# A fused attention and feed-forward kernel whose hand-listed order of operations is replaced by another order

## The chip, the cores and the metric

The kernel runs on one core of a Trainium2 chip. The metric is the device time of one execution in microseconds (us), of which smaller is better. A core has TensorE (PE in the profile, with its weight loads as PEld), VectorE (DVE), ScalarE (ACT), GpSimd (POOL) and SyncE (SP). TensorE writes its products into PSUM, eight banks of accumulators, and only VectorE and ScalarE read them out in this kernel.

## The reference: what is computed

Attention with a squared ReLU in the place of softmax, over 8 batches and 12 heads of 448 rows and 64 columns, and then a feed-forward block with an exact GELU over the 3584 rows of 768 columns:

```python
scores = scale * np.matmul(q, k.transpose(0, 1, 3, 2))
attn = np.maximum(scores, 0.0) ** 2 / S
x = np.matmul(attn, v)        # laid out as 3584 x 768
h = x @ w_in                  # 768 x 2048
g = 0.5 * h * (1.0 + erf(h / sqrt(2)))
out = g @ w_out               # 2048 x 768
```

## The kernel before: how the work is laid out

The kernel first records its work as 1,596 operations of a class `Op` (some of which, like a product, are up to 28 instructions) and then issues them one by one from a table. The kinds that matter here are these.

- **Transposes.** For batches 0 and 1 TensorE turns k and q (`tp`, L619 and L647) and a copy takes them out of PSUM into `kT` and `qT` (L518 when VectorE copies, L520 when ScalarE does). From batch 2 on a DMA on SP's queue turns them (L674).
- **Scores.** A step is four products `ps` of 64x64 blocks (L751), a scaled ReLU out of PSUM into `a_sq` (L768 on ScalarE, or L770 on VectorE) and a squaring on VectorE (L777). Seven steps feed the 28 products `pav` (L824), and two copies take `pav` out into `xT` (L518 or L520).
- **First layer.** Batch 0 uses plain products `psh` (L884) and a GELU (L894). Batches 1 to 6 use a scheme of seven block products in the place of eight (`add_unit`: products `pe` at L1039, copies and additions `part` out of PSUM at L518, L520 and L1077, GELU at L1089). Batch 7 has the like in `add_block` (`pb`, L1190 and L1227).
- **Second layer.** Groups of 256 rows, again with seven block products (`pso`, L1366, additions L1400, sums of operands L1347), and stores on SP's queue (L1319, L1327).

PSUM is divided into two pools. `w_pp` (tag "w") has three tiles of two banks each, here called pairs: a `ps`, a `pav`, a `pe` or a `pb` takes one pair. `f_pp` (tag "f") has two single banks, for `tp`, `psh`, `pso`. An operation marked Q in the table takes the two single banks in the place of a pair (`split`).

In `add_unit` two units of work share each pair. Unit y=0 uses the first bank and unit y=1 the second:

```python
if first and name not in bank:
    bank[name] = w_pp.tile([128, 2, NB], F32, tag="w", name="pe")
...
bank[name][:, y, z * HS : z * HS + HS],
```

Each unit runs product after product into its banks, and the next product into a bank waits for the copy or addition (`passed`) that took the former value out. So there is a chain in each unit: product, copy, product, copy. The other unit's products stand between and give the copy its time. Where the copies of the two units are given to two engines, the built program carries a semaphore wait between them, since both read one tile, the pair: the later of the two in the table waits for the earlier.

The order is a list of words in the table `ORDER` at the top of the file. The letter gives the engine (P and Q TensorE, A ScalarE, D VectorE, G GpSimd, S SyncE, Z a filler on TensorE) and the number the operation. `place()` goes through the words, and `run()` issues the operations in that order, so each engine's instruction stream is the table's words with its letter, read in sequence. Each engine takes its stream strictly in order: an instruction that waits holds back all that stand behind it.

```python
for word in ORDER.split():
    ...
    op, eng = self.open[int(word[1:])], names[word[0]]
    if word[0] == "Q":
        op.split()
```

Of the kernel before, what the change touches and what calls it, by code (L numbers as in the profile page):

```python
# [83 lines left out]
A10 D13 G0 G1594 Z1024 P14 P11 D15 G1 G3 G4 G7 D12 A16 P17 P36 D18 A37 P21 G118 G2 P19 P42 P39 P33  # L84
D22 G117 P23 D20 A43 D40 P48 A34 A49 D24 P25 P54 A55 D26 Z672 P63 P66 D38 A67 D41 D50 P51 A52 P29
D35 P27 D28 D30 D44 P57 D53 D68 P31 D32 A64 A58 P131 P81 G121 A82 P45 A46 A47 P69 A70 D132 D59 G6
P129 P84 A85 P90 A91 G125 G126 D65 G5 D130 P156 D71 D157 P78 A79 Q72 D73 P93 A94 P102 D83 G8 G122
G120 G124 G119 G128 P111 D112 P137 D113 P108 A74 D95 G123 G9 G127 D138 G236 P174 D56 A103 A109 P139
D86 P75 A175 A76 D110 D140 P133 P60 P105 D77 P96 A61 A62 P168 A106 G235 D80 P135 D136 D104 A97 P171
G238 A172 P87 D134 P141 G147 G148 G150 D92 A169 A88 A89 A142 P159 A160 D98 P162 P99 D107 D163 G151  # L90
Q114 A100 A101 P198 A199 D115 D116 P183 A184 P165 A166 D176 P145 A146 S228 S229 G153 P240 A241 D173
D158 G154 D200 P213 A214 P180 D170 A181 P222 P252 A253 D167 S230 P250 A251 D223 P195 D161 A196 P207
D164 D208 P177 P186 A187 D182 D209 D178 D179 P210 D197 P262 A263 D215 A211 G234 P256 P192 D193 P189
P216 P254 A190 A257 S231 P219 A255 D191 D349 D350 D212 P204 A220 P244 S232 S233 D194 A217 P248 A245
A249 D218 D185 P260 A205 P242 A243 D188 P201 A202 D224 G237 G149 G152 A261 G155 D221 D206 P225 D387
D226 D203 A227 D345 D346 D348 P246 A247 D351 P264 G239 G266 P353 P370 A354 P360 P143 A144 G267 P377
P356 D425 D426 A371 D427 A361 A378 D347 P258 A259 D352 P373 D388 P382 P355 A374 P379 D383 D380 P372
P365 A357 P362 D358 P385 A386 D375 A359 D366 D363 P391 P408 A364 G268 P368 A369 P398 P415 P393 P410
D431 A265 D428 A399 D389 P403 D390 A409 A392 P394 D413 P411 A416 P420 D396 D432 A384 A367 P282 Q273
A412 D395 G269 P400 P417 D421 A274 D404 A405 P437 A283 A422 A438 P276 A277 D433 S453 D418 D401 S454  # L100
D434 P291 D429 D435 A292 P406 P423 A424 D430 A407 A402 P439 G270 P288 A289 P285 A286 D293 P297 D298
D440 P441 A442 P315 A316 P279 D284 A414 D287 D436 P300 D290 P443 D444 D275 A280 D281 P445 P447 D278
P309 A301 D446 D448 S451 A397 G271 P303 A419 A381 P294 A376 D469 D470 S455 A310 D295 A304 S456 S457
S458 D305 P312 D311 P449 D450 S452 A313 D302 D314 A296 P321 D471 A322 D323 P324 A325 P306 A307 D308
D317 P473 A474 P339 G459 P327 A328 P475 P477 P336 D299 G462 D472 A340 D329 D476 A337 D338 A478 P330
P318 A331 G272 P333 D334 A319 A320 D332 P479 P498 A499 P492 G465 D341 P489 A490 P481 A493 P495 A496
D335 D326 P342 A343 P507 P504 A505 D480 D482 P485 D344 D561 D562 D564 D563 A508 P565 G460 G461 D509
P582 A583 P572 P589 D494 P585 D586 P567 P584 D500 A566 P568 D573 P591 D570 A590 D592 P594 D587 P577
D599 A569 P483 D578 G463 P601 A588 P618 D486 D595 A602 P574 P597 A598 G464 D600 D491 G466 G467 D575
P603 A576 P620 D484 D619 S488 P580 A581 S635 D606 D497 Q501 A593 S636 A502 S637 D623 P604 P621 D506  # L110
D503 A622 P608 P625 A624 A605 D651 D652 P513 A514 D515 Q510 P522 P610 S638 A596 P627 D626 D628 G641
G644 A609 P613 D611 D653 P630 A511 A512 A523 A571 D614 Q516 A517 P519 D520 P616 P633 D631 A632 D654
D524 A617 P655 A634 P657 P528 D656 D529 P531 A532 D533 S487 G468 P549 A550 D658 P659 D521 A607 D518
P543 A544 P540 A660 D541 P537 A538 P661 P663 D662 A579 D539 P694 P555 D530 D551 A629 P525 A612 A526
D664 A695 D545 D527 P665 D666 A556 D542 P667 A615 D671 P709 A710 D672 P534 P546 S669 P706 A547 D535
A536 A707 P675 D668 P677 P552 S639 S640 G647 P703 D696 P691 D673 G642 D676 D674 D678 P679 A680 D553
A692 P681 D548 D557 P697 D554 P558 G643 G645 G646 D708 A704 P715 D698 P700 D682 D559 P683 A701 D560
P767 P784 D684 D763 A716 D785 A768 D705 D764 P687 P769 P786 P774 D711 D766 P787 A788 D765 A775 D772
P685 A773 G648 D693 D688 D789 G649 S690 P770 A771 D699 P791 D686 P779 A790 Q727 D728 P724 S837 S838
A792 D702 A725 P793 P776 D794 A795 P796 P803 P820 D777 S839 P799 S840 A778 G843 P782 D801 D797 A800  # L120
A783 D804 S670 Q712 P718 G846 D821 D780 A798 A719 A713 A714 P805 P822 P806 D802 P823 D825 A824 Q748
P721 D808 P810 D729 P827 A807 P812 D726 A749 A828 D722 P757 Q730 P829 A811 D717 D853 D854 D830 S689
D813 A731 S841 P832 D833 P857 D858 A826 P818 D732 P815 A809 P835 D720 D816 D855 A831 A819 P859 D860
A758 D759 P861 A817 D862 A836 A834 P896 A897 P733 P739 D740 P863 D856 A734 P742 P905 A906 P745 P865
D898 D864 D866 G650 P867 D735 D750 A781 P869 D868 D723 D870 S872 A814 D873 D874 S842 A746 D747 P920
A921 P736 A737 D738 P751 D876 A743 D744 A752 D753 P877 P879 P911 P754 A878 D880 D875 D741 P908 A755
D756 P881 A882 D909 A912 D922 P883 P893 D894 D884 P899 A900 D910 D895 P760 P926 A761 A762 P923 A924
P885 D886 G849 P887 P902 D913 D901 G844 D888 D965 A927 D967 A903 P917 D907 P889 D890 P969 P986 G845
G847 G848 A918 S1039 D904 Q935 D936 P929 A970 A930 P914 A915 A916 Q941 P971 P988 D966 D968 D919 P976
P993 D925 A987 D991 G850 A994 D937 P972 P989 A990 D977 G851 P981 S892 S1040 D974 A942 P998 A973  # L130
D1003 P1005 P1022 D999 A1000 A1023 P978 D982 D979 A1006 P1007 P1024 D1027 P1008 A992 S1041 A980 Q932
D1010 P995 A1028 P1025 A1026 A933 D996 A997 D1009 P1012 P1029 A1030 D1004 D934 P1014 P1031 D1032
A975 D1013 P1001 A1002 D1015 P1059 D1060 P984 A1016 A985 D931 A1033 S871 G1045 P1020 P1037 A1038
P1034 D1057 P1017 A1021 P950 P1098 P1063 D1055 D1056 D1018 S891 A983 D1035 D951 S1042 S1043 G1048
A1019 P1061 P959 A1099 D1100 P956 D928 D1062 A957 D960 A1036 P938 A939 A940 P1101 D1102 P944 A945
D1058 D946 P1065 A1064 P947 P953 P1119 A1011 D1066 D961 P1067 D958 G852 A948 D1068 A1120 P1069 D943
P1095 A954 D955 D1070 A1096 D1097 D949 D1075 D952 P1122 P1125 A1126 S1073 A1123 P1071 D1072 D1076
P1079 D1080 P1128 D1078 S1074 P1107 A1108 P962 D963 A964 P1110 P1081 D1082 P1083 A1129 A1084 P1104
D1077 D1111 S1044 G1051 G1046 P1113 A1114 P1085 P1173 D1112 A1105 D1106 D1169 P1087 D1109 P1190
P1171 P1188 A1172 A1189 D1086 D1088 P1091 D1103 D1167 D1168 P1178 D1170 D1176 D1092 P1195 A1196  # L140
P1089 P1174 P1191 D1193 A1194 D1130 D1090 Q1134 A1177 A1135 D1115 P1116 D1124 D1179 D1127 A1192
Q1143 D1117 P1183 D1118 A1144 P1200 P1137 A1138 D1175 Q1131 D1201 D1184 A1185 G1047 G1049 P1197
P1180 A1132 A1202 G1050 D1205 D1181 A1182 D1198 D1206 S1241 P1207 P1224 D1208 P1209 P1226 A1225
Q1155 A1156 A1199 P1186 D1212 P1210 D1229 D1145 P1203 A1230 A1204 D1133 P1227 D1228 A1211 P1214
P1231 A1187 P1216 P1233 Q1146 D1139 A1213 D1121 A1232 A1147 D1136 P1140 A1141 Q1149 A1142 D1215
P1219 P1236 D1217 A1218 D1234 A1235 D1150 D1237 A1238 P1222 P1239 G1052 D1220 S1242 Q1152 A1223
D1153 A1240 G1053 A1221 P1270 A1271 P1279 A1280 S1093 S1094 P1276 P1251 A1252 P1158 P1161 D1247
S1243 D1248 A1277 P1253 D1249 D1162 D1157 A1159 P1255 D1254 D1160 P1257 S1244 D1148 D1256 P1259
P1267 P1273 A1274 D1163 D1154 D1151 D1258 D1260 A1268 D1250 P1164 A1165 D1278 P1285 D1281 A1166
D1339 D1340 P1263 A1286 S1245 P1345 P1343 P1360 A1361 P1350 D1272 P1367 P1362 D1287 D1342 D1344  # L150
A1351 P1346 A1368 P1363 A1364 P1372 A1347 D1365 P1261 A1366 D1341 D1275 D1348 P1352 P1369 D1370
D1353 P1355 D1356 S1246 G1595 P1379 P1396 G1054 P1358 D1373 A1371 A1357 D1262 P1375 A1374 A1380
D1377 D1378 P1381 P1398 D1264 D1384 A1397 P1382 P1399 A1359 A1376 A1383 P1386 P1403 A1349 D1401
# [1551 lines left out]
```

## Time and profile before

| | |
|---|---|
| time, median of 3 runs | 365.86 us (365.82 to 366.21) |
| profiled execution, its own time | 365.36 us |
| its span, first to last instruction | 363.5 us |
| mean granted TensorE clock | 0.999 |
| instructions in the span | 9,137 |
| chain that ended last: TensorE | 83% of the span |
| chain that ended last: VectorE, ScalarE, DMA | 8%, 4%, 2% |

The profiled execution is 0.50 us faster than the median of the three timed runs, of which 1.9 us lie outside the span. A row of the timeline gives a start from the span's first instruction, a duration, the engine, the line of the kernel, the operation, its output and input with their shapes, and how many instructions were merged into the row. In brackets stand the idle time ahead of it on its engine and what ended that. A row of the waits view gives who waited for whom, the sum, the count and the longest. A row of the windows view gives, for a stretch of time, the length and then busy time and number of instructions for PE, PEld, DVE, ACT and POOL, and last the TensorE clock, the DMA share and GB/s.

### The profile page before, as it was taken

What the parts mean: (1) busy time and instruction counts of PE and PEld (TensorE: products, weight loads), DVE (VectorE), ACT (ScalarE), POOL (GpSimd) and SP (SyncE); (2) the same over time, 40 slices, a digit from 0 to 9 for tenths busy, and PEclk for the clock granted to TensorE, in tenths of its full rate; (3) what the DMA queues carried; (4) which work ended last, traced back from release to release, by engine and by line L of the source; (5) the groups of instructions that cost most, each with busy time, mean ns of one, the idle gap of its engine ahead of it and who ended that gap; (6) DMA issues with size and microseconds to landing.
All of it is one profiled execution on the core that took longest, in us unless ns stands there. A gap on an engine that the chain in (4) does not pass through costs nothing.

```text
span 363.5 us, 9137 instructions
## 1 busy us (share of the span) xinstructions
PE 352.7 (97%) x3805; PEld 244.2 (67%) x3805; DVE 312.9 (86%) x544; ACT 233.4 (64%) x396; POOL 102.9 (28%) x138
## 2 busy tenths in 40 slices
PE   8889999999999999999999999999999999999995
PEld 4557569855588655886557975678669855798663
DVE  3999988999789899899999799899896999687753
ACT  4998844899846795567675869457854885344200
POOL 8565715284192105610074100470100000000000
PEclk9999999999999999999999999999999999999999
DMA  9999999999999808997199941699900201021213
GB/s 176 200 200 204 202 204 155 172 143 168 155 161 173 157 21 107 142 208 107 56 81 167 183 74 45 94 129 181 136 2 0 88 2 44 3 88 43 88 43 132
DMA packets 124361, 43.01 MB, mean 118 GB/s; under 512 B 102688, under 2 KB 120992, under 8 KB 124320
## 3 DMA queue, kind: packets, MB, share of 16 engines
q0 software_dynamic: 85328, 22.47, 66.4%
q1 hardware_dynamic: 38448, 19.50, 26.3%
q8 instruction: 30, 0.49, 0.6%
q10 hardware_dynamic: 544, 0.46, 0.4%
q14 instruction: 11, 0.09, 0.1%
HBM read 45.61 MB, written 11.01 MB: 156 GB/s over the span
## 4 chain that ended last, share of the span: by engine, by line
PE 83%; DVE 8%; ACT 4%; DMA 2%; issue 1%; POOL 1%; DVEq 0%; POOLq 0%; ACTq 0%
PE pso L1366 36%; PE pe L1039 21%; PE ps L751 8%; PE pav L824 8%; PE psh L884 5%; PE pb L1190 4%; DVE a_sq L777 2%; DMA nq<-in_q_dram 2%; DVE part L1077 2%; DVE part L518 2%; ACT part L520 2%; ACT h_sb L1089 1%; ACT a_sq L768 1%; DVE qT L518 1%; DVE ws L955 0%
## 5 line engine op out<-in xcount | busy, mean ns | idle before, releaser
L768 ACT ACTIVATE a_sq<-ps 128x896 bf16<-128x896 f32 (+1 forms) x151 | 121.9, 861 | 26.1 <-PE ps L751 25.3
L777 DVE TENSOR_TENSOR a_sq<-a_sq 128x896 bf16<-128x896 bf16 x169 | 98.2, 615 | 1.9 <-ACT a_sq L768 1.5
L1366 PEld LDWEIGHTS <-s_sb 128*128 128x128 bf16 x456 | 42.5, 98 | 31.9 <-issue 6.0
L1039 PEld LDWEIGHTS <-win_sb 128*128 128x128 bf16 x576 | 54.4, 98 | 7.9 <-issue 6.3
L751 PE MATMUL ps<-qT,kT 64*64 64x448 bf16 (+1 forms) x756 | 50.0, 338 | 2.4 <-DVE kT L518 0.8
L1077 DVE TENSOR_TENSOR part<-pe,part 128x448 f32<-128x448 f32 x72 | 42.4, 618 | 7.6 <-PE pe L1039 5.9
L1366 PEld LDWEIGHTS <-h_sb 128*128 128x128 bf16 x336 | 31.8, 98 | 22.6 <-issue 4.1
L520 ACT COPY part<-pe 128x448 f32<-128x448 f32 x54 | 27.5, 535 | 29.7 <-PE pe L1039 20.6
L1089 ACT ACTIVATE h_sb<-part 128x448 bf16<-128x448 f32 x72 | 39.9, 580 | 8.8 <-DVE part L1077 8.7
L1039 PEld LDWEIGHTS <-ws 128*128 128x128 bf16 x432 | 41.2, 98 | 2.9 <-issue 2.0
L1366 PE MATMUL pso<-wout_sb,s_sb 128*128 128x384 bf16 (+2 forms) x232 | 41.1, 321 | 0.0
L1366 PE MATMUL pso<-wout_sb,h_sb 128*128 128x384 bf16 x224 | 41.1, 327 | 0.0
L1366 PE MATMUL pso<-t_sb,s_sb 128*128 128x384 bf16 x224 | 41.1, 326 | 0.0
L558 POOL DMA_DIRECT2D nk<-in_k_dram x36 | 34.7, 968 | 10.4 <-DMA wout_sb<-in_moe_w_out_dram 7.9
L770 DVE TENSOR_SCALAR a_sq<-ps 128x896 bf16<-128x896 f32 (+1 forms) x35 | 33.5, 967 | 4.7 <-PE ps L751 4.1
L824 PE MATMUL pav<-a_sq,v_sb 64*64 64x448 bf16 (+1 forms) x756 | 36.4, 329 | 0.5 <-ACT a_sq L768 0.4
L751 PEld LDWEIGHTS <-kT 64*64 64x64 bf16 x756 | 19.0, 105 | 23.8 <-issue 17.9
L1039 PE MATMUL pe<-t_x,win_sb 128*128 128x224 bf16 x288 | 32.6, 259 | 1.3 <-DVE part L518 0.6
L1039 PE MATMUL pe<-t_x,ws 128*128 128x224 bf16 x288 | 31.2, 259 | 0.4 <-ACT part L520 0.4
L708 POOL COPY gate<-qT 128x16 bf16<-128x16 bf16 x10 | 3.0, 299 | 101.1 <-DMA qT<-nq 101.1
L1039 PE MATMUL pe<-xT,win_sb 128*128 128x224 bf16 x288 | 31.5, 259 | 0.0
L1400 DVE TENSOR_TENSOR osb<-pso,p_sb 128x384 f32<-128x384 f32 x42 | 23.2, 552 | 8.8 <-PE pso L1366 7.8
(71 smaller groups left out, 411.8 us busy)
## 6 DMA issues: line engine op xcount, KB each, us to landing
out_dram<-osb SPq DMA_DIRECT2D x19, 384.0 KB, 2.6
nq<-in_q_dram POOLq DMA_DIRECT2D x38, 112.0 KB, 5.9
nk<-in_k_dram POOLq DMA_DIRECT2D x36, 112.0 KB, 5.6
v_sb<-in_v_dram POOLq DMA_DIRECT2D x5, 672.0 KB, 7.5
v_sb<-in_v_dram POOLq DMA_DIRECT2D x9, 224.0 KB, 7.9
win_sb<-in_moe_w_in_dram POOLq DMA_DIRECT2D x8, 192.0 KB, 8.7
wout_sb<-in_moe_w_out_dram POOLq DMA_DIRECT2D x4, 384.0 KB, 12.6
wout_sb<-in_moe_w_out_dram POOLq DMA_DIRECT2D x1, 1536.0 KB, 15.6
```

The lines of the kernel that those rows point to most:

```text
L520: A.copy(dst, src)
L558: nc.gpsimd.dma_start(nk[b][:, g0, :, e], rows[:, e].rearrange("p (i d) -> p i d", d=D))
L751: nc.tensor.matmul(side(ps, e)[64 * j : 64 * j + 64, x * w : x * w + w], kT[r, g, i * 128 + 64 * j : i * 128 + 64 * j + 64], moving, start ...
L768: A.activation(to, x, AF.Relu, scale=c_att)
L770: V.tensor_scalar(to, x, c_att, 0.0, op0=mybir.AluOpType.mult, op1=mybir.AluOpType.max,)
L777: V.tensor_mul(box["a2"][:, :, :used], ar, ar)
L824: nc.tensor.matmul(side(pav[0], e)[o2 : o2 + 64, :w], vt[b][r, 2 * g + e, bass.ts(i, D)], box["a2"][r, e, o : o + w], start=(i == 0), stop ...
L1039: nc.tensor.matmul(bank[name][:, y, z * HS : z * HS + HS], w[:, k, bass.ts(mm, 128)], right()[:, k], start=first and k == 0 and z == 0, st ...
L1077: V.tensor_add(get(to), ps(name), get(other))
L1089: A.activation(h_ring()[:, m : m + 2, o + half[c].start : o + half[c].stop], src().rearrange("p (x n) -> p x n", x=2), AF.Gelu,)
L1366: nc.tensor.matmul(box[bank][:, n0:n1], left()[:, kf], right()[:, kf, n0:n1], start=bool(need) and kf == 0, stop=kf == K2 - 1, skip_group_ ...
L1400: V.tensor_add(out()[:, n0:n1], box[bank][:, n0:n1], other()[:, n0:n1])
```

## The change

Only the table `ORDER` differs. The same 1,596 operations are issued, in another order. The first words of the table before and after (the rest of it differs in the same way):

```diff
-A10 D13 G0 G1594 Z1024 P14 P11 D15 G1 G3 G4 G7 D12 A16 P17 P36 D18 A37 P21 G118 G2 P19 P42 P39 P33
...
-D1585 S1590
+A10 D13 G0 G1594 Z1024 P14 P11 D15 G1 G3 D12 G4 A16 P17 P36 A37 P19 D18 P42 A43 G7 D20 P21 D22 D38
...
+S1590
```

Counted over the table:

| | before | after |
|---|---|---|
| TensorE operations, of them split (Q) | 523, 22 | 523, 15 |
| ScalarE operations | 381 | 395 |
| VectorE operations | 537 | 523 |
| moved from VectorE to ScalarE, and the other way | | 62, 48 |
| changes on TensorE between 64x64 and 128x128 products | 115 | 111 |
| pairs of `pe`, two readers in a row on two engines | 55 | 43 |
| pairs of `pe`, two readers in a row on one engine | 77 | 89 |
| pairs of `pav`, copies on two engines | 8 | 4 |
| GpSimd's sequence | | unchanged |

**Place one: the first unit pair of batch 2 in the first layer.** These rows are ScalarE's stream before, where three of the rows read the pair `pe_2031`; `part` is the copy in SBUF, `pe` the PSUM pair, and "waits DVE" or "waits PE" names the engine whose semaphore the instruction waits for.

```order
L520 COPY part_2049<-pe_2031 128x448 [waits PE_49]
L520 COPY part_2087<-pe_2031 128x448 [waits DVE_49]
L520 COPY part_2104<-pe_2051 128x448 [waits DVE_49]
L520 COPY part_2121<-pe_2031 128x448 [waits DVE_49]
L1089 ACTIVATE h_sb_818<-part_2049 128x2x224 [waits DVE_49]
```

And these are VectorE's at the same place before.

```order
L777 TENSOR_TENSOR a_sq_1956<-a_sq_1956 128x896
L518 COPY part_2071<-pe_2031 128x448 [waits PE_49,Activation_49]
L777 TENSOR_TENSOR a_sq_1931<-a_sq_1931 128x896
L518 COPY part_2095<-pe_2051 128x448
L1077 TENSOR_TENSOR part_2087<-pe_2073,part_2087 128x448 [waits PE_49,Activation_49]
```

In the changed kernel the pair is `pe_2024`, and VectorE has the first two copies out of it:

```order
L518 COPY part_2038<-pe_2024 128x448 [waits PE_49]
L998 TENSOR_TENSOR t4_x_2054<-xT_1766,t2_x_2022 128x672 [waits DVE_49]
L518 COPY part_2071<-pe_2024 128x448
L1077 TENSOR_TENSOR part_2071<-pe_2041,part_2071 128x448 [waits DVE_49,PE_49]
L1400 TENSOR_TENSOR osb_1991<-pso_1842,p_sb_1797 128x384 [waits PE_49]
L777 TENSOR_TENSOR a_sq_1937<-a_sq_1937 128x896
L1077 TENSOR_TENSOR part_2038<-pe_2041,part_2038 128x448
L518 COPY part_2117<-pe_2024 128x448 [waits Activation_49]
```

Before, the readings out of `pe_2031` went ScalarE, VectorE, ScalarE, and the second ScalarE copy (`part_2087`) waited for VectorE's. Now the copies out of the fresh pair, `part_2038` and `part_2071`, stand on one engine without a wait between them; of the later readings, `part_2117` on VectorE waits for a copy of ScalarE.

**Place two: the first unit pair of batch 4 in the first layer.** ScalarE's stream before, where `pe_3556` is the pair `c` of that batch:

```order
L520 CAST xT_3529<-pav_3500 128x448
L520 COPY part_3570<-pe_3457 128x448 [waits DVE_49]
L520 COPY part_3575<-pe_3556 128x448 [waits PE_49]
L520 COPY part_3590<-pe_3457 128x448 [waits DVE_49,PE_49]
L768 ACTIVATE a_sq_3605<-ps_3532 128x448 [waits DVE_49]
```

VectorE's stream before:

```order
L777 TENSOR_TENSOR a_sq_3476<-a_sq_3476 128x896 [waits Activation_49]
L777 TENSOR_TENSOR a_sq_3403<-a_sq_3403 128x896
L1077 TENSOR_TENSOR part_3570<-pe_3538,part_3570 128x448 [waits PE_49,Activation_49]
L777 TENSOR_TENSOR a_sq_3488<-a_sq_3488 128x896
L518 COPY part_3592<-pe_3556 128x448 [waits Activation_49]
```

ScalarE's stream in the changed kernel, where that pair is `pe_3544`:

```order
L768 ACTIVATE a_sq_3495<-ps_3482 128x896 [waits DVE_49]
L520 COPY part_3527<-pe_3507 128x448 [waits PE_49]
L520 COPY part_3566<-pe_3544 128x448 [waits PE_49]
L520 COPY part_3569<-pe_3544 128x448 [waits DVE_49]
L768 ACTIVATE a_sq_3576<-ps_3571 128x896 [waits PE_49]
L520 COPY part_3597<-pe_3507 128x448 [waits DVE_49,PE_49]
```

The two copies out of the pair `c` stood on ScalarE and VectorE, the second waiting for the first; now both stand on ScalarE, one behind the other.

**Place three: ScalarE's stream while the kernel starts up, before,** between the copies of batch 0's `xT` and the second `psh`:

```order
L520 CAST xT_427<-pav_673 128x224
L768 ACTIVATE a_sq_728<-ps_702 128x896 [waits PE_49]
L768 ACTIVATE a_sq_751<-ps_712 128x896 [waits DVE_49,PE_49]
L768 ACTIVATE a_sq_760<-ps_753 128x896 [waits PE_49]
L768 ACTIVATE a_sq_814<-ps_723 128x896 [waits DVE_49,PE_49]
L520 CAST xT_427<-pav_762 128x224 [waits PE_49]
L520 CAST xT_427<-pav_762 128x224
L894 ACTIVATE h_sb_818<-psh_792 128x2x224 [waits PE_49]
```

The same stretch in the changed kernel:

```order
L520 CAST xT_457<-pav_611 128x224 [waits PE_49]
L768 ACTIVATE a_sq_659<-ps_651 128x896 [waits PE_49]
L768 ACTIVATE a_sq_666<-ps_661 128x896 [waits DVE_49,PE_49]
L520 COPY kT_380<-tp_671 128x896 [waits PE_49]
L894 ACTIVATE h_sb_700<-psh_687 128x2x224 [waits PE_49]
L768 ACTIVATE a_sq_715<-ps_710 128x896 [waits PE_49]
L768 ACTIVATE a_sq_747<-ps_702 128x896 [waits DVE_49,PE_49]
L768 ACTIVATE a_sq_772<-ps_767 128x896 [waits PE_49]
L520 COPY kT_380<-tp_774 128x896 [waits PE_49]
L520 CAST xT_457<-pav_717 128x224
```

Two copies of `kT` that VectorE had are now ScalarE's, a third, of `qT`, stands earlier in the same stream, and the GELU of the first `psh` comes five operations sooner. VectorE in turn has four ReLUs ahead of that GELU in the place of three, and seven of the twelve `xT` copies of batch 0 in the place of three.

## The prediction on record

> **What bounds the kernel now.** I read the page's busy times first, then its chain, then the windows by stage. A window row gives the stretch, its length, and the busy time of PE, PEld, DVE, ACT and POOL.
>
> ```profile
> PE 352.7 (97%) x3805; PEld 244.2 (67%) x3805; DVE 312.9 (86%) x544; ACT 233.4 (64%) x396; POOL 102.9 (28%) x138
> PE 83%; DVE 8%; ACT 4%; DMA 2%; issue 1%; POOL 1%; DVEq 0%; POOLq 0%; ACTq 0%
> 5.00:14.00 9.00, 7.57 (x193) 5.23 (x192) 7.63 (x17) 7.56 (x11) 6.97 (x10) 1.00 1.47 191
> 14.00:27.00 13.00, 10.73 (x291) 7.36 (x288) 12.53 (x24) 12.62 (x20) 8.15 (x12) 1.00 1.32 201
> 27.00:53.00 26.00, 26.00 (x325) 16.20 (x325) 23.63 (x40) 19.68 (x33) 13.04 (x17) 1.00 1.30 203
> 100.00:122.00 22.00, 21.45 (x228) 18.23 (x227) 20.02 (x36) 13.56 (x26) 12.37 (x15) 1.00 1.61 171
> 233.00:260.00 27.00, 26.56 (x291) 21.18 (x292) 24.47 (x45) 17.91 (x36) 11.20 (x14) 1.00 1.57 138
> ```
>
> TensorE is the bound nearly everywhere. The exception is the start-up to 27 us: from 14 to 27 us VectorE is busy 12.53 and ScalarE 12.62 of 13 us, while PE has gaps. There the readers of PSUM set the pace. Behind it PE is short of work only in small holes, in the stages of the first layer (`pe`), such as 100 to 122 us.
>
> A reordering leaves PE's products as they are. So its worth is what it removes of two things: PE's waits, and the cost of changing between 64x64 products (attention) and 128x128 products (feed-forward). A wait is read from PE's starts, since a busy time contains the pipelining: from the start of one run of products to the next, less the spacing of such products times their number. Read so over the whole stream, PE loses 7.7 us up to 27 us and 4.9 us behind it.
>
> **The change, term one: the turns.** PE's timeline and the timeline of all engines at one of the holes:
>
> ```profile
> 101.95 0.53 ACT L520 COPY part<-pe 128x448 f32<-128x448 f32 x1 [0.79 <-PE pe L1039]
> 103.47 1.31 PE L1039 MATMUL pe<-xT,win_sb 128*128 128x224 bf16 x12
> 103.74 0.62 DVE L518 COPY part<-pe 128x448 f32<-128x448 f32 x1 [0.50 <-PE pe L1039]
> 104.40 0.53 ACT L520 COPY part<-pe 128x448 f32<-128x448 f32 x1 [1.92 <-DVE part L518]
> 104.99 0.73 PE L1039 MATMUL pe<-t_x,ws 128*128 128x224 bf16 x6 [0.20 <-ACT part L520]
> ```
>
> This is place one of the change. VectorE's copy out of the pair runs from 103.74 to 104.36. ScalarE, which had been idle since 102.48, starts its copy out of the pair's other bank at 104.40, 0.04 us behind VectorE's end, and PE starts 0.05 us behind that copy. From the end of the product that VectorE reads (PE's next run starts at 103.47) to PE's restart the path is 0.27 + 0.62 + 0.04 + 0.54 + 0.05 = 1.52 us. PE has 12 products in between, which are spaced 0.096 us (six take 0.57, next fence), so 1.15 us. It stands for 1.52 - 1.15 = 0.37 us.
>
> I went through the table before for every product that waits for a copy which itself waits for a reader on the other engine, and counted PE's work between the end of the product that the first reader needs and the waiting product. In eight places it is 1.15 us; the next are at 1.7 us and more. At all eight PE stands in the trace. The first and the last of them:
>
> ```profile
> 60.30 0.74 PE L1039 MATMUL pe<-xT,win_sb 128*128 128x224 bf16 x6
> 60.87 0.74 PE L1039 MATMUL pe<-xT,ws 128*128 128x224 bf16 x6
> 61.74 1.12 PE L1039 MATMUL pe<-t_x,win_sb 128*128 128x224 bf16 x10
> 252.06 1.89 PE L1039 MATMUL pe<-t_x,ws 128*128 128x224 bf16 x18
> 254.13 1.31 PE L1039 MATMUL pe<-t_x,win_sb 128*128 128x224 bf16 x12 [0.19 <-ACT part L520]
> ACT part L520 <- DVE part L518: 6.2, 6, 1.9
> DVE part L518 <- ACT part L520: 2.6, 6, 0.6
> ```
>
> Six products from 60.87 end at 61.45, PE restarts at 61.74: 0.29 us. Eighteen from 252.06 end at 253.78, restart at 254.13: 0.35 us. The eight together are 2.7 us. The waits rows confirm the pairs: ScalarE waits for VectorE's `part` copies and the other way, 12 times.
>
> In the changed table no product has a lead of 1.15 us behind a turn. The shortest are 1.59 us for one pair of `pav`, and 1.72, 1.73, 1.87 and 2.3 us for `pe`, against a need of 1.52. Place one now has 2.3 us, and at place two both copies stand on ScalarE. So all eight holes should close: **-2.7 us**, between -2.7 and 0.
>
> Here a page of the Trainium skill speaks against the change. "PSUM — Partial Sum Buffer", section Specifications (TRN2), quotes that ScalarE and VectorE can access PSUM in parallel at full bandwidth as long as there is no bank collision. By that, readers of the two banks of a pair need no turns, and a reorder could win nothing there. The trace differs: ScalarE's 1.92 us of idle time end 0.04 us behind VectorE's copy of the other bank. That is a wait of this program, whatever the banks allow.
>
> **Term two: fewer changes of product shape.** PE at a stretch that alternates:
>
> ```profile
> 86.81 0.36 PE L751 MATMUL ps<-qT,kT 64*64 64x448 bf16 x4
> 87.11 1.47 PE L1366 MATMUL pso<-wout_sb,h_sb 128*128 128x384 bf16 x8
> 88.51 0.57 PE L751 MATMUL ps<-qT,kT 64*64 64x448 bf16 x8
> 89.02 1.47 PE L1366 MATMUL pso<-t_sb,s_sb 128*128 128x384 bf16 x8
> 90.33 1.46 PE L1366 MATMUL pso<-wout_sb,h_sb 128*128 128x384 bf16 x8
> ```
>
> Eight `pso` ahead of another `pso` take 1.31 us (89.02 to 90.33), ahead of a `ps` 1.40 (87.11 to 88.51): 0.09. One step of `ps` ahead of `pso` takes 0.30 and two take 0.51, so 0.21 each and 0.09 to 0.1 for the change. There were 115 such changes and are 111: **-0.4 us**. This hides behind nothing, since PE is the bound.
>
> **Term three: the start-up.** VectorE's spacings from its own timeline, and the rows that fix the end of the stage:
>
> ```profile
> 8.35 1.08 DVE L770 TENSOR_SCALAR a_sq<-ps 128x896 bf16<-128x896 f32 x1
> 9.35 0.61 DVE L518 COPY kT<-tp 128x896 bf16<-128x896 bf16 x1
> 9.88 0.38 DVE L518 COPY qT<-tp 128x448 bf16<-128x448 bf16 x1
> 10.18 2.22 DVE L777 TENSOR_TENSOR a_sq<-a_sq 128x896 bf16<-128x896 bf16 x4
> 26.71 1.69 DVE L777 TENSOR_TENSOR a_sq<-a_sq 128x896 bf16<-128x896 bf16 x3
> 8.04 7.06 ACT L768 ACTIVATE a_sq<-ps 128x448 bf16<-128x448 f32 x9 [0.38 <-PE ps L751]
> 6.98 0.24 PEld L647 LDWEIGHTS <-nq 112*64 112x64 bf16 x8 [0.54 <-DMA nq<-in_q_dram]
> 30.68 2.41 PE psh L884 x24
> ```
>
> So VectorE needs 1.00 us for a ReLU, 0.53 for a large copy, 0.30 for a small one and 0.54 for a squaring; ScalarE about 0.8 for a ReLU. In both orders 56 operations with 20.2 us of PE work stand ahead of the second `psh`, which started at 30.68. In the new order the last of them wait for an `xT` copy on VectorE, behind 22 squarings, four ReLUs and 18 other copies. Summed from VectorE's first copy at 5.5 us, that is 28.6 us. In the trace of before VectorE fell 0.5 to 1.2 us behind such a sum by 28 us (the three squarings that end at 28.40 come out at 27.1). So 29.1 to 29.8 us. Behind the copy come a score product (0.2), its ReLU (0.24 to start, 0.9), whose pair the last score product needs (0.2), and the change of shape (0.1): the second `psh` at 30.8 to 31.5, 0.1 to 0.9 us later. Against that the transposition that waited for its DMA at 6.98 now stands behind a score step, so ScalarE's second ReLU can start some 0.3 us sooner. I take **+0.3 us**, between -0.6 and +1.4, the upper end if ScalarE's two `kT` copies also fall on the path.
>
> **Term four: other waits of PE behind 27 us.** Nine more, read the same way, sum to 2.2 us. The two largest:
>
> ```profile
> 250.91 0.73 PE L1039 MATMUL pe<-t_x,ws 128*128 128x224 bf16 x6 [0.25 <-ACT part L520]
> 260.74 0.38 PE L751 MATMUL ps<-qT,kT 64*64 64x448 bf16 x4 [0.38 <-ACT h_sb L1089]
> ```
>
> At 260.74 a score product waits for a pair that a GELU frees: PE's work in between was 0.67 us, and is 0.48 in the new order, so it gets about 0.2 worse. The others are queues of a busy engine, which the new order deals anew; VectorE, the fuller one, loses 14 operations to ScalarE net. I take **-0.3 us**, between -1.5 and +1.0.
>
> **Edits at no cost.** ScalarE's 14 more operations (some 7 us) hide in its slack, 19.68 busy of 26 us even in its fullest stage behind the start-up. The stores on SP's queue change places with the transposing DMAs:
>
> ```profile
> kT<-nk SPq DMA_TRANSPOSE x18, 6.6
> SPq L1319 <- DVE osb L1400: 137.8, 16, 25.1
> ```
>
> SP does stand up to 25.1 us for a store's data with transposes behind it. But in the new table the PE work between a store's last product and the first use of the next transpose is 19.6 us or more everywhere (18.9 before), and a transpose lands 6.6 us after its issue. If that cover went, PE would wait the rest.
>
> **The sum.** -2.7 - 0.4 + 0.3 - 0.3 = -3.1 us: 362.3 for an execution like the profiled one (365.36), which is 0.5 below the median of the runs, so **362.8** beside 365.86.
>
> **Rivals.** *Queues take the place of turns.* The leads of 1.59 to 1.87 us exceed the need by only 0.1 to 0.35 us. One VectorE operation of 0.62 us ahead of the copy eats that. Speaking for it: VectorE is 91% busy from 100 to 122 us. Against it: the ScalarE copies at these leads meet an engine with slack. With 0.3 us lost at four such places, and term four at +0.2, the sum is -2.7 + 1.2 - 0.4 + 0.3 + 0.2 = -1.4: 364.5.
>
> *The turns are no waits.* If the late copies were late for a reason of their own, nothing at the eight holes would close: -0.4 + 0.3, so 365.8. The PSUM page's rule would give this. The 0.04 us at 104.40, and the like at the other seven, speak against it.
>
> *The start-up gives it all back (slower).* There ScalarE has no slack, and it takes two `kT` copies and one `qT` copy, some 0.8, 0.8 and 0.5 us (estimates from ScalarE's 0.53 for 448 columns), with a VectorE that waits for its ReLUs. If all that comes on the path, and each late ReLU holds a squaring (0.54) that a `pav` waits for, the stage ends 2.1 + 3 x 0.54 = 3.7 us later, against the +0.3 taken. Then the sum is +0.3, with another 0.5 where term four turns bad: 366.5. It decides from a delay of the second `psh` of 3.4 us on. The four ReLUs that VectorE takes over speak against it.
>
> **How the numbers follow.** The forecast gets 0.72, queues 0.18, no turns 0.05, and a start-up that gives back more than the rest brings 0.05, of which 0.01 ends within the band. The forecast's own bounds run from about 361.3 (terms three and four at their good ends are unlikely together) to 364; the range adds the queues, to 364.7. A measurement of this kernel can tell some 0.2%, 0.7 us. Faster by more: 0.90 (forecast and queues); within: 0.06; slower: 0.04.
>
> **What would show it.** In the profile of the changed kernel: PE's starts at the `pe` products of place one and two without a hole; the waits rows between ScalarE's and VectorE's `part` copies may stay, but not as PE's wait. The second `psh` at 30.7 to 31.5 us. PE's hole by a GELU near 258 us, 0.5 to 0.9 us long. I am wrong if new holes of 0.3 us appear at the `pe` products with leads near 1.8 us, or if the second `psh` starts past 32 us.

## The result and the profile after

| | before | after |
|---|---|---|
| median of the runs | 365.84 us | 361.00 us |
| profiled execution, its own time | 365.36 us | 360.84 us |
| its span | 363.5 us | 358.8 us |
| changes of product shape on PE | 115 | 111 |
| start of the second `psh` | 30.61 us | 30.42 us |
| PE's waits behind it: the eight turns | 2.7 us | 0 |
| PE's waits behind it: all others | 2.2 us | 0.8 us |

The ratio is 0.9875 (95% interval 0.9848 to 0.9902): the gain is 4.8 us, where 3.1 was forecast. The waits are read from PE's starts as in the prediction; PE's last run of products started at 358.35 us and now starts at 353.71, 4.64 us earlier. (The prediction's 30.68 us for the second `psh` is a row of the chain; the timeline has 30.61.)

The page's busy times, its chain, and the windows by stage, for the changed kernel (columns as before):

```profile
PE 350.5 (98%) x3805; PEld 244.7 (68%) x3805; DVE 304.2 (85%) x529; ACT 240.1 (67%) x403; POOL 104.9 (29%) x138
PE 93%; ACT 3%; DVE 3%; issue 0%; DVEq 0%
14.00:27.00 13.00, 11.10 (x284) 8.19 (x285) 13.00 (x26) 13.00 (x20) 7.31 (x11) 1.00 1.32 201
100.00:122.00 22.00, 22.00 (x240) 18.77 (x238) 19.96 (x35) 14.66 (x30) 11.28 (x13) 1.00 1.70 157
233.00:260.00 27.00, 26.51 (x297) 20.34 (x298) 25.39 (x47) 20.42 (x37) 5.80 (x8) 1.00 1.13 141
```

The chain is now 93% TensorE (83% before). From 100 to 122 us PE is busy without a gap; from 233 to 260 it isn't yet. From 14 to 27 us VectorE and ScalarE have no idle time left at all: 13.00 of 13 us each.

Place one in the changed kernel, four of PE's and VectorE's rows of its timeline:

```profile
101.09 0.62 DVE L518 COPY part<-pe 128x448 f32<-128x448 f32 x1
102.04 0.62 DVE L518 COPY part<-pe 128x448 f32<-128x448 f32 x1
102.94 1.46 PE L1366 MATMUL pso<-t_sb,h_sb 128*128 128x384 bf16 x8
104.24 0.45 PE L1039 MATMUL pe<-t_x,ws 128*128 128x224 bf16 x3
```

The two copies end at 102.66, and the product that needs them starts at 104.24, just 1.30 us behind the start of eight `pso`, which is their spacing. No hole is left. Nor is there one at place two: its two copies end at 196.74 us, and the product into the first bank starts at 197.91.

What is left behind the start-up is one place, the GELU of the prediction:

```profile
254.32 1.32 PE L1039 MATMUL pe<-t_x,win_sb 128*128 128x224 bf16 x12
254.67 0.90 ACT L768 ACTIVATE a_sq<-ps 128x896 bf16<-128x896 f32 x1
254.73 1.15 DVE L518 CAST xT<-pav 128x448 bf16<-128x448 f32 x2
255.68 0.98 ACT L1089 ACTIVATE h_sb<-pe 128x448 bf16<-128x448 f32 x2
255.98 0.57 PE L751 MATMUL ps<-qT,kT 64*64 64x448 bf16 x8 [0.34 <-PE pe L1039]
256.71 0.38 PE L751 MATMUL ps<-qT,kT 64*64 64x448 bf16 x4 [0.16 <-ACT h_sb L1089]
```

Less the 0.1 us for the change of shape, PE waits 0.40 us at 255.98 and 0.33 us at 256.71, 0.73 us in all. The first product waits for a pair that VectorE's second `pav` copy frees (it ends at 255.88), the second for the pair of the two GELUs, which end at 256.66. The GELU sets the whole: PE's work between the pair's last product and the one at 256.71 is 0.5 us as forecast, so without the first wait the second would be 0.73.

### The profile page after: what moved, and what is told of

Read it like the earlier page. It is cut to its first block, busy times and chain, and to the rows that moved or that the text cites. A ratio compares the mean times of both kernels' runs of the same rounds, so it can differ in the third digit from the quotient of the medians.

```text
span 358.8 us, 9136 instructions
## 1 busy us (share of the span) xinstructions
PE 350.5 (98%) x3805; PEld 244.7 (68%) x3805; DVE 304.2 (85%) x529; ACT 240.1 (67%) x403; POOL 104.9 (29%) x138
## 3 DMA queue, kind: packets, MB, share of 16 engines
q1 hardware_dynamic: 38448, 19.50, 27.1%
## 4 chain that ended last, share of the span: by engine, by line
PE 93%; ACT 3%; DVE 3%; issue 0%; DVEq 0%
PE pso L1366 37%; PE pe L1039 27%; PE ps L751 10%; PE pav L824 8%; PE psh L884 5%; PE pb L1190 4%; ACT a_sq L768 2%; PE spin L1501 1%; DVE a_sq L777 1%; DVE a_sq L770 1%; DVE qT L518 1%; PE tp L619 0%; DVE kT L518 0%; ACT h_sb L1089 0%; PE fill L1667 0%; ACT xT L520 0%
## 5 line engine op out<-in xcount | busy, mean ns | idle before, releaser
L768 ACT ACTIVATE a_sq<-ps 128x896 bf16<-128x896 f32 (+1 forms) x148 | 124.6, 897 | 25.1 <-PE ps L751 24.6
L770 DVE TENSOR_SCALAR a_sq<-ps 128x896 bf16<-128x896 f32 (+1 forms) x30 | 29.5, 993 | 3.4 <-PE ps L751 3.3
L476 POOL DMA_DIRECT2D nq<-in_q_dram x36 | 30.0, 838 | 2.3 <-DMA wout_sb<-in_moe_w_out_dram 2.1
```

The source lines that it names most:

```text
L476: nc.gpsimd.dma_start(nq[b][:, g0, :, e], rows)
L768: A.activation(to, x, AF.Relu, scale=c_att)
L770: V.tensor_scalar(to, x, c_att, 0.0, op0=mybir.AluOpType.mult, op1=mybir.AluOpType.max,)
```

## The experiments

### Turning the turns round

First, the order before with the two readers of a pair in the other order at the eight places: each engine's stream stays as it was. What changes is the direction of the wait between the two engines; at some places a few words of the one engine had to move past words of the other as well. The first of the eight:

```diff
-P379 D383 D380 P372 P365 A357 P362
+P379 D383 A357 D380 P372 P365 P362
```

> The kernel before with eight pairs of words changed in the table, so that at the eight places with a lead of 1.15 us the copy that PE waits for stands ahead of the other reader of its pair; every engine's stream stays as it was, and only the direction of the wait between the two readers turns. Turn theory: the eight holes close, 2.7 us less than before, some 363.1 us beside 365.8. Rival (the copies are late for a reason of their own, such as the queue of their engine): nothing changes, 365.8 within 0.4.

Measured: 366.82 us, ratio 1.0035 (1.0023 to 1.0046). No hole closed, and 1.25 us were lost (the kernel before had 365.57 us beside it), which neither expectation had. The eight holes come to 3.0 us in the place of 2.7, and new ones came, the largest of 0.48 us at 107.07. The first place in its timeline:

```profile
59.96 0.74 PE L1039 MATMUL pe<-t_x,win_sb 128*128 128x224 bf16 x6
60.73 0.53 ACT L520 COPY part<-pe 128x448 f32<-128x448 f32 x1 [1.16 <-PE pe L1039]
61.30 1.16 DVE L1077 TENSOR_TENSOR part<-pe,part 128x448 f32<-128x448 f32 x2 [0.80 <-ACT part L520]
61.98 0.54 PE L1039 MATMUL pe<-t_x,win_sb 128*128 128x224 bf16 x4
```

ScalarE's copy is out of the first bank, whose own product was done more than 3 us before. It starts at 60.73 all the same, 0.2 us behind the end (60.53) of the product into the *second* bank. VectorE's reading of that bank follows it (its row holds two readings; this one, the first, ends at 61.92), and PE's product into the first bank starts at 61.98, 0.06 us behind the end of VectorE's reading, of a bank that it doesn't write. So the rule of this program is wider than the prediction had it: **the pair is one unit**. A reader waits for every product into either bank that stands ahead of it in the table, and for the other engine's readers; a product waits for every reader of both banks. The chain product, reader, reader, product is as long whichever reader is first.

The second run turned two more places round, at 119.02 and 250.91 us, which the prediction had put under "other waits":

```diff
-P627 D626 D628 G641 G644 A609 P613
+P627 A609 D626 D628 G641 G644 P613
...
-P1224 D1208 P1209 P1226 A1225 Q1155
+P1224 A1225 D1208 P1209 P1226 Q1155
```

> The same with two more pairs changed, at the products that started at 119.02 and 250.91 us, which the prediction had put down to queues (0.30 and 0.42 us of PE's waits). If they are turns too: 0.7 us below the run with eight, 3.4 us below before, some 362.4. If they are queues of a busy engine: the same as with eight.

Measured: 365.97 us, ratio 1.0009 (0.9997 to 1.0021). That is 0.85 us below the run with eight, where two more turns were expected to bring 0.7. These two holes did close, the eight stayed. The reason stands in the order before:

```profile
116.58 0.69 DVE L1347 TENSOR_TENSOR s_sb<-s_sb,h_sb 128x1024 bf16<-128x1024 bf16 x1
117.19 0.62 DVE L777 TENSOR_TENSOR a_sq<-a_sq 128x896 bf16<-128x896 bf16 x1
117.73 0.61 DVE L518 COPY part<-pe 128x448 f32<-128x448 f32 x1
118.43 0.53 ACT L520 COPY part<-pe 128x448 f32<-128x448 f32 x1 [0.83 <-DVE part L518]
248.81 0.95 DVE L955 TENSOR_TENSOR ws<-win_sb,ws 128x1536 bf16<-128x1536 bf16 x1
249.68 0.62 DVE L518 COPY part<-pe 128x448 f32<-128x448 f32 x1
250.33 0.53 ACT L520 COPY part<-pe 128x448 f32<-128x448 f32 x1 [0.96 <-DVE part L518]
```

At both places VectorE's copy was late because it queued behind a sum or a squaring, and ScalarE, idle for 0.83 and 0.96 us, waited for it. There the direction matters: with ScalarE first, its copy goes while VectorE is still busy. These are two more turns, of 0.30 and 0.42 us; a busy queue had made them long.

### Mending by the wider rule

If the pair is one unit, the way out is to take the late reader off the path between the other bank's product and the waiting product. Three places were mended so, and the two exchanges that had worked were added:

```diff
-A361 A378 D347 P258 A259 D352 P373 D388 P382 P355 A374 P379 D383 D380 P372 P365 A357 P362
+A357 A378 D347 P258 A259 D352 P373 D388 P382 P355 A374 P379 D383 D380 P372 A361 P365 P362
...
-P385 A386 D375 A359 D366 D363 P391 P408 A364 G268 P368 A369
+P385 D375 A359 D366 D363 P391 P408 A364 G268 P368 A386 A369
...
-D1010 P995 A1028 P1025 A1026 A933 D996 A997 D1009
+D1009 D1010 P995 A1028 P1025 A1026 A933 D996 A997
```

> The order before, with five of its places mended after the refined rule: a product into either bank of a pair waits for every reader of both banks that stands ahead of it in the table, and every reader waits for all products and for the other engine's readers ahead of it. So the way out is to take the late reader off the path between the other bank's product and the waiting product. Place 61.74 us: ScalarE's copy out of the waiting bank goes three copies forward, into the idle 3 us behind its own product. Place 64.34: the GELU of the other bank goes behind the waiting product. Place 207.72: VectorE's copy goes ahead of another bank's addition. The two places at 119.02 and 250.91 get the exchange that closed them before. Refined rule: those five holes close (0.29 + 0.30 + 0.35 + 0.30 + 0.42 = 1.66 us), one new wait of 0.08 us near 58 us, the five holes at 70.6, 105.0, 112.3, 200.1, 254.1 us stay: 1.6 us faster than before, 364.2 us beside 365.8. Rival, the copies are late for a reason of their own, whatever stands around them: only the two places of the earlier run close, 0.7 us.

Measured: 364.03 us, ratio 0.9959 (0.9946 to 0.9972), 1.6 us faster. All five holes closed, and the five others stayed (0.48, 0.36, 0.30 and 0.29 us, and the last, at 252.55, grew from 0.35 to 0.61). The first place:

```profile
58.06 0.73 PE L1039 MATMUL pe<-t_x,ws 128*128 128x224 bf16 x6
60.95 0.73 PE L1039 MATMUL pe<-xT,ws 128*128 128x224 bf16 x6
61.52 1.12 PE L1039 MATMUL pe<-t_x,win_sb 128*128 128x224 bf16 x10
```

From 60.95 to 61.52 is the spacing of six products: no hole. The new wait of 0.08 us that was expected came at 58.06, and one as long at 65.63.

### Opening holes in the changed kernel

The opposite test: in the changed order four pairs of neighbouring products change places, which cuts PE's lead to 1.15 us.

```diff
-P601 P591
+P591 P601
...
-P832 D816 P818
+P818 D816 P832
...
-P978 D1010 A975 A933 A983 S1040 D1027 G851 P1008
+P1008 D1010 A975 A933 A983 S1040 D1027 G851 P978
...
-P1231 P1203
+P1203 P1231
```

> The changed order with four pairs of neighbouring products on TensorE exchanged, so that 1.15 us of products in the place of 1.72 stand behind the product that the first reader of a pair needs. Nothing else is moved. At two of the places the two readers are on two engines, at the two others both are on VectorE. Refined rule (the lead counts, not which engine reads): four new holes, worked out from the reader's ends in the trace of the changed kernel: 0.29 us near 106.5, 0.34 near 201.4, 0.38 near 250.8 and 0.29 near 163.2: 1.3 us slower than the changed kernel, 362.3 beside 361.0. Rival, only a handover between two engines costs: the first two alone, 0.6 us. Rival, leads of 1.15 us are no bound: nothing.

Measured: 363.28 us, ratio 0.9933 (0.9921 to 0.9945). All four holes opened: 0.29 us at 106.03, 0.31 at 162.99, 0.35 at 202.73, 0.33 at 252.94. One of the two places where both readers are on VectorE:

```profile
251.46 1.31 PE L1039 MATMUL pe<-t_x,win_sb 128*128 128x224 bf16 x12
251.73 1.16 DVE L518 COPY part<-pe 128x448 f32<-128x448 f32 x2 [0.37 <-PE pe L1039]
252.94 0.83 PE L1039 MATMUL pe<-xT,ws 128*128 128x224 bf16 x7 [0.16 <-DVE part L518]
```

Two copies on one engine end 1.16 us behind 251.73, and PE stands 0.33 us, as long as with two engines. So it isn't the handover that costs, but two readings behind one product with 1.15 us of PE work beside them. Some 1.3 us of the slowdown are these holes. Another 1.29 us came in a way that was not expected:

```profile
162.85 0.68 DVE L1347 TENSOR_TENSOR s_sb<-h_sb 128x1024 bf16<-128x1024 bf16 x1
163.57 0.69 DVE L1347 TENSOR_TENSOR s_sb<-s_sb,h_sb 128x1024 bf16<-128x1024 bf16 x1
164.18 0.62 DVE L1077 TENSOR_TENSOR part<-pe,part 128x448 f32<-128x448 f32 x1
164.85 0.73 PE L1039 MATMUL pe<-xT,ws 128*128 128x224 bf16 x6 [1.12 <-DVE part L1077]
```

The exchange had put product 832 behind the addition 816 in the table. 816 reads the pair's other bank, so 832 now waits for it, and 816 stands behind two sums of operands on VectorE. This is the wider rule at its dearest.

### Relieving VectorE, and single queues

VectorE loses 14 operations in the new order. Is it that which closes the holes? Here the order before keeps its sequence of words, with the engine letters of the new one (110 letters):

```diff
-D40
+A40
...
-D26
+A26
...
-A52
+D52
```

> The kernel before in its own order, but with the 110 operations given to ScalarE or VectorE as the changed kernel gives them. Turn theory: three holes of 1.15 us lead stay, the others close for the most part (two copies in a row on ScalarE need 1.3 us, on VectorE 1.5), so 1.0 to 1.8 us less than before. Rival (the gain comes from relieving VectorE, whichever the order): the larger part of the whole 4.8 us, more than 2.4.

Measured: 398.95 us, ratio 1.0933 (1.0902 to 1.0965). Letters without their order make things far worse: the second `psh` comes at 37.75 us in the place of 30.61, PE is busy for 91% of the span (97% before), and it waits over the whole run for readings that now stand in the wrong place of a stream. Neither expectation came, so the run doesn't tell what a lighter VectorE alone is worth.

Then three single waits of term four, each by moving what PE waits for ahead of one operation of its own engine:

```diff
-A544 P540 A660
+A660 A544 P540
...
-D1292 D1389
+D1389 D1292
...
-D1548 P1543 D1544
+P1543 D1544 D1548
```

> The order before, with three operations moved ahead of one that stood before them on their own engine, at three of the nine waits of term four: VectorE's copy that TensorE waits for at 288.93 ahead of a ReLU, ScalarE's copy out of the bank waited for at 129.09 ahead of a ReLU, VectorE's addition out of the bank waited for at 342.76 ahead of a sum of operands. Theory (queues of a busy engine, a place of its own each): those three holes close, 0.30 + 0.12 + 0.12 = 0.5 us faster, 365.3 beside 365.8, all other holes as they were. Rival (the engine has no time to give, so what is put behind is waited for in its turn): a new wait of about the same length within 3 us of each place, and 0 in all.

Measured: 366.20 us, ratio 1.0011 (1.0002 to 1.0020). The holes at 129.09 and 288.93 closed (0.12 and 0.30 us), the one near 343 stayed at 0.12, now for the sum that was put behind. And near 290 three new waits came, 0.75 us together:

```profile
291.27 1.15 DVE L1077 TENSOR_TENSOR part<-pe,part 128x448 f32<-128x448 f32 x2
291.94 0.38 PE L751 MATMUL ps<-qT,kT 64*64 64x448 bf16 x4 [0.30 <-DVE part L1077]
292.48 0.73 PE L1039 MATMUL pe<-t_x,win_sb 128*128 128x224 bf16 x6
```

The score product at 291.94 waits 0.45 us for a pair that VectorE's additions free, and the product at 292.48 waits 0.25 us for the second of these; they stand behind the ReLU that was put back. So the rival held at the two places on VectorE, which is busy for 28.98 of the 33 us from 260 to 293 in the order before: there one queue mended alone is paid back a few us on. At the place near 129, on ScalarE, nothing came back. Why the new order can close the same waits was not tried; everything behind them moves too.

### The start-up apart from the rest

Two splices: the order before up to the second `psh` (not with it) and the new order for what is left, and the other way round.

```diff
 A166 D176
-P145 A146 S228
+P186 A187 D158
```

> The first words of the table from the kernel before, up to just behind the second psh, and the rest in the changed kernel's order. If the start-up brought little: 361.0 to 361.5 us (the changed kernel's 361.0 and some 0.2 to 0.5). If the start-up is what made the gain larger than forecast: 361.8 or more.

```diff
 D173 P177
-D205 G148 P180
+G148 G150 G151
```

> The changed order up to the second psh, and behind it the order before. Forecast's view (start-up and rest are independent, the start-up is worth 0.2 us as read from the two profiles, the rest keeps its 4.9 us of waits): 365.5 us beside 365.8. Rival, the start-up of the changed order is worth what the opposite splice lacked (363.4 against 361.0): 363.4 us. Rival, the seam itself costs: over 366, with waits of TensorE of over 0.3 us behind 30 us that neither kernel has.

Measured: the old start with the new rest 363.41 us, ratio 0.9941 (0.9926 to 0.9956); the new start with the old rest 369.08 us, ratio 1.0103 (1.0086 to 1.0120). The rows of the seam, first of the one and then of the other:

```profile
31.12 3.34 ACT L768 ACTIVATE a_sq<-ps 128x896 bf16<-128x896 f32 x4 [0.21 <-PE ps L751]
32.09 0.38 PE L751 MATMUL ps<-qT,kT 64*64 64x448 bf16 x4 [0.64 <-ACT a_sq L768]
33.71 0.38 PE L751 MATMUL ps<-qT,kT 64*64 64x448 bf16 x4 [0.43 <-ACT a_sq L768]
```

```profile
39.55 0.38 PE L751 MATMUL ps<-qT,kT 64*64 64x448 bf16 x4 [1.02 <-ACT a_sq L768]
40.95 0.38 PE L751 MATMUL ps<-qT,kT 64*64 64x448 bf16 x4 [1.01 <-ACT a_sq L768]
```

The seam itself costs, as the second splice's last rival had it. In both a score product waits for a ReLU to free its pair, three times in a row: 2.0 us from 32 to 34 in the first, 3.3 us from 39 to 46 in the second. Away from the seam the rests behave as at home: 0.7 us of waits with the new rest, and with the old one 4.8 us with every hole of the order before at its place. So the 4.1 us between the rests are shown to be the rest's own; the start-up's worth can't be had from the splices, since a start fits only the steps that follow it.

### The place that is left

In the changed order, the ReLU ahead of the two GELUs goes to VectorE and the first `pav` copy to ScalarE:

```diff
-P1149 D1141 D1142 P1222 P1239 D1148 A1150
+P1149 D1150 A1141 D1142 P1222 P1239 D1148
```

> The changed order with two operations near 254 us given to the other engine: the ReLU that stands ahead of the pair's two GELUs goes to VectorE, and the first copy of a pav to ScalarE. In the profile of the changed kernel TensorE waits 0.40 us at 255.98 for the pair that VectorE's second pav copy frees, and 0.33 us at 256.71 for the pair that the second GELU frees, which had queued behind that ReLU. If that queue is the cause, the GELUs end some 0.4 us sooner and the two holes together shrink from 0.73 to 0.3 to 0.4 us: 360.7 beside 361.0. Rival: VectorE has the ReLU late too, the pair it frees is the one that the next score step needs, and nothing is gained or up to 0.4 us lost there.

Measured: 360.97 us, ratio 0.9870 (0.9858 to 0.9883), the same as the changed kernel. The holes there are 0.71 us in the place of 0.73:

```profile
254.54 1.32 PE L1039 MATMUL pe<-t_x,win_sb 128*128 128x224 bf16 x12
255.90 0.98 ACT L1089 ACTIVATE h_sb<-pe 128x448 bf16<-128x448 f32 x2 [0.50 <-PE pe L1039]
```

ScalarE is now idle for 0.50 us ahead of the GELUs, and the first starts at 255.90 all the same, 0.2 us behind the end of twelve products (254.54 + 1.15 = 255.69), though six are its own. In the changed kernel it was 255.68, with 254.32 + 1.15 = 255.47. So the ReLU wasn't what held it. It waits for the product into the other bank, which stands ahead of it: the wider rule once more. The ReLU, now late on VectorE, holds up a score product at 256.08 instead, as the rival had it.

## Why the forecast fell short, point by point

Of the 1.7 us between -3.1 and -4.8, term four is 1.1 us (forecast -0.3, measured -1.4) and term three 0.5 us (forecast +0.3, measured -0.2). The step that failed above all is the size of term four; the other is what stands behind the last copy in term three.

- **Term one, the turns: right in size, too narrow in its reason.** All eight holes closed: -2.7 us as forecast, and the count of leads named the right eight. But the prediction took the wait between two engines for the cause. The runs show a pair treated as one unit, and what decides is PE's work between the last product into either bank and the waiting product; two copies on one engine cost as much.
- **Term two, changes of shape:** 111 as counted. The -0.4 us was not measured apart; of the 4.64 us at PE's last run, 0.35 us are left when the waits (4.1) and the second `psh` (0.19) are taken off, which fits.
- **Term three, the start-up: wrong sign, if inside its bounds.** Forecast +0.3 us with the second `psh` at 30.8 to 31.5; measured 30.42 against 30.61, -0.2 us in this pair of profiles. The sum for VectorE held: its last copies before that point end at 29.8, the late end of 29.1 to 29.8. What failed is the sentence "Behind the copy come a score product (0.2), its ReLU (0.24 to start, 0.9), whose pair the last score product needs". The trace of the changed kernel:

```profile
28.57 0.36 PE L751 MATMUL ps<-qT,kT 64*64 64x448 bf16 x4
28.79 0.99 DVE L518 CAST xT<-pav 128x224 bf16<-128x224 f32 x3
28.98 1.07 ACT L768 ACTIVATE a_sq<-ps 128x896 bf16<-128x896 f32 x1
29.70 0.79 PE L751 MATMUL ps<-qT,kT 64*64 64x448 bf16 x12
30.42 1.32 PE L884 MATMUL psh<-xT,win_sb 128*128 128x224 bf16 x12
```

  The ReLU that frees the last pair (28.98 to 30.05) belongs to a product of 28.57 and runs beside the copies, not behind them. The `psh` starts 0.64 us behind the copies in the place of 1.64. From one profile to the next this point also moves by itself: with this start-up it came at 29.68, 30.09, 30.42 and 30.80 in four kernels, with the old one at 30.60 to 31.11 in five. The means are 30.25 and 30.80, so as an estimate the new start-up is worth rather -0.5 us.
- **Term four, the other waits: mis-sized, and the larger part of the miss.** "I take -0.3 us, between -1.5 and +1.0"; measured -1.4 (2.2 to 0.8). Two of the nine, 0.72 us, were turns: the count began each chain 0.27 us behind its product, so it missed those whose first reader was itself late in VectorE's queue. The hole by the GELU came as forecast (0.73, of 0.5 to 0.9, from 0.52). The six others, 1.0 us, were taken for queues, and all closed, while a new one of 0.07 came: 0.7 + 1.0 - 0.2 - 0.1 = 1.4. That two of three such queues can't be mended alone was shown; that the order as a whole closes them is read from its trace, and what in the order does it stays open.
- **The range.** It ended at 361.3 because "terms three and four at their good ends are unlikely together". Term four came to its good end and term three near it, and 361.0 lay just below. The good ends of all terms sum to -2.7 - 0.4 - 0.6 - 1.5 = -5.2 us, 360.7: the range was cut short of the prediction's own bounds. Why both should go well together was not tried.
- **The rivals.** Queues in the place of turns: no hole came at the leads of 1.59 to 1.87 us. "The turns are no waits" fell with the eight. The rule behind it, of the Trainium skill's page "PSUM — Partial Sum Buffer", section Specifications (TRN2), that ScalarE and VectorE can access PSUM in parallel as long as there is no bank collision, isn't refuted by that: in none of these chains did the program let two engines read one pair at once, so no run here shows what the two banks of a pair would allow. Readers of different PSUM tiles do run at once: in the order before, 22 of ScalarE's 54 copies out of `pe` overlap a reading of VectorE from another PSUM tile, and take 0.53 us on average, as the other 32 do. There the trace agrees. The start-up gave nothing back.
- **Two slips in the sums**, which bear on no reading: the slower rival's terms come to +0.8 us, 366.7 and not 366.5, and VectorE's squarings lay 1.3 us behind the sum (28.40 against 27.1), not up to 1.2.

## What to carry to other kernels

Find what the program treats as one unit (here a pair of banks in one tile) before counting waits: every reader and writer ahead in the issue order counts, in all of it. Then count, for each product, the engine's own work between the last writer that its readers wait for and the product itself, start each chain where its first reader's queue lets it start, and compare with the chain (here 1.5 us with two readers). A hole mended alone on an engine as full as VectorE here (88% busy near 290 us) may only move; ask what stands behind the operation that is put back.

## What the runs showed beyond that

With the letters alone the granted clock of TensorE fell to about half of full speed in four stretches of the profiled execution, near 12 to 19, 26 to 29, 60 to 64 and 289 to 292 us. The windows of that kernel around the last two (columns as before, the clock third from the end):

```profile
56.80:60.20 3.40, 1.60 (x28) 0.86 (x31) 3.40 (x7) 0.66 (x3) 3.16 (x4) 0.99 2.39 155
60.20:63.60 3.40, 3.40 (x31) 1.57 (x31) 1.34 (x3) 0.91 (x3) 1.18 (x2) 0.51 2.00 141
285.50:288.90 3.40, 0.98 (x20) 0.38 (x12) 2.73 (x6) 0.00 (x0) 0.00 (x0) 0.99 0.82 131
288.90:292.30 3.40, 3.32 (x19) 2.69 (x19) 2.06 (x5) 2.19 (x5) 0.00 (x0) 0.51 0.00 0
```

Ahead of both PE was short of work, 1.60 and 0.98 us busy of 3.40; whether that lowered the clock wasn't tried. The profiled execution, the slowest of six, took 401.93 us at a mean clock of 0.979, where the profiles of all other kernels here have 0.998 or more. The fastest took 398.39 us at 0.996, still 32.8 us more than the kernel before, so all but a few us of the slowdown are not the clock's.
